# Attention into a two-layer feed-forward kernel: the first half step's product split into two stages, and the start-up issued in another order

## The chip, the cores and the metric

The kernel runs on one core of a Trainium2 chip. The metric is the device time of one execution in microseconds (us). TensorE is called PE, VectorE DVE, ScalarE ACT, GpSimd POOL, and SyncE, which issues the DMAs, SP. "SBUF" is the memory on the chip, "PSUM" the memory that PE writes.

## The reference, cut to what matters

```python
# q, k, v: (4, 8, 768, 64); mem_k, mem_v: (4, 8, 8, 64)
for c in range(24):                       # chunks of 32 tokens
    q_c = q[:, :, c_start:c_end]
    k_ctx = k[:, :, max(0, c_start - 16):min(S, c_end + 8)]
    k_full = concatenate([mem_k, k_ctx], axis=2)          # 64 keys
    scores = scale * q_c @ k_full.T
    a = exp(scores - max(scores)); a = a / (sum(a) + 1e-9)
    out[:, :, c_start:c_end] = a @ v_full
x = out.transpose(0, 2, 1, 3).reshape(3072, 512)
h = x @ w_in                              # 512 -> 2048
g = where(h >= 1, h, where(h <= -1, 0, (h + 1) ** 2 / 4))
return g @ w_out                          # 2048 -> 512
```

Everything is float32. The kernel gets that precision from PE by splitting x, g and the weights into a high and a low part (`hi`, rounded to a shorter format, and `lo`, the rest) and adding three products: high by high, high by low, low by high.

## The kernel before, in words

The 3072 tokens are six blocks of 512. For a block, attention makes x in SBUF as `xth` and `xtl` (high and low part, 512 features as four slices of 128 by 512 tokens). Then come 16 steps, one for each slice `fc` of 128 hidden columns: a *product* (`ps_h`, 12 matmuls: 8 that read `xth`, against the high and the low part of the weights, then 4 that read `xtl`), a *gate* (three ACT operations out of PSUM, a sum on DVE, a cast on ACT that gives the high part `gh`, a subtraction on DVE that gives the low part `gl`), and an *out* (`ps_o`, adding to the block's 512x512 result in four PSUM banks).

The first two blocks are issued by hand: `FIRST` (line 32) is a list of names, and for every name the loop at line 551 advances one generator by one stage, up to its next `yield`. Since every engine runs its instructions in the order of issue (`InOrder`, line 55), the list is the order on each engine; where a name stands matters only against other names with stages on the same engine. A wait on an engine therefore holds all that stands behind it there. The names are:

- `g0` to `g3` (`first_attention`, line 212): attention of block 0 in four groups, one for each half of the tokens (g0 and g1 the first half) and each half of the features (g0 and g2 the first two slices). The 13 stages: scores (PE, 64 matmuls), maximum, subtraction (DVE), exponential (ACT), row sum, +1e-9, reciprocal, multiplication (DVE), transposes (PE, 4), copy `pt` (ACT), values (PE, 64 matmuls), cast to `xth` (ACT), subtraction to `xtl` (DVE).
- `n0` to `n3` (`attention`, line 369): the same for the halves of blocks 1 and 2, all heads at once (128 matmuls each for scores and values); here the transposition is six DVE operations, and the scores and the values use one PSUM place, tag `s`, in turn. So n1's scores wait until n0's last subtraction to `xtl` has read it.
- `w0` to `w15` (`decode`, line 148): the weights come packed and are unpacked in place. Stages: scaling (ACT), shift, two merges (DVE), cast to the high part (ACT), subtraction to the low part (DVE). w0 holds the first two `fc` of w_in; w1 holds `fc` 2 of w_in and `fc` 0 of w_out, and so on.
- `A0` to `A3`, `B0` to `B3`: half steps of block 0, `fc` 0 to 3, for tokens 0 to 255 (A) and 256 to 511 (B); `J4` to `J15`: whole steps. C, D and E are the same for block 1. All are `early_step` (line 452), with the stages product, gate, sum, cast, subtraction, out (and stores after `fc` 15). A0 needs x of g0 and g1 only, B0 that of g2 and g3.
- `+`: the next load of the list `early` (line 530), on SP.

The products use a pool of two PSUM banks, `ps_h`, in the order of issue; g's transposes use it too. After `FIRST` a regular loop (line 573) runs blocks 2 to 5. What the change touches is `FIRST` and lines 464 and 465 in `early_step`.

Of the kernel before, what the change touches and what calls it, by code (L numbers as in the profile page):

```python
# [29 lines left out]


FIRST = """
    + + g0 g0 + g0 g1 g0 + g0 g1 g1 g0 g0 + g1 g0 w0 g1 g0 + g1 g1 g1 g0 w0 g1 + w0 g2 g1 w0 g1 g2 +
    w0 g2 w1 g0 w0 + g2 w1 g1 g2 + g0 g2 g2 g2 + g0 g2 w1 g3 g2 g1 w1 + A0 w2 g3 w1 g3 A1 w2 + g3 w1
    w3 g3 g2 A0 g3 g3 + A1 g3 A2 w2 g2 w4 g3 g2 A2 A0 w2 g3 A0 + g3 w3 w2 A0 w3 A0 g3 g3 + w2 B0 A1
    w3 A3 A1 B0 + A1 w3 B0 B1 w4 B0 w3 A3 A1 + B1 B0 w4 w5 B2 B1 w6 A2 w4 n0 + A2 B1 A2 w4 B1 A2 A3
    w5 A3 B2 + A3 w5 B3 w8 B2 w7 B0 w4 + B2 w5 B3 A3 w9 B2 B3 B1 w6 B3 + w5 w6 J4 w10 B3 w5 + w6 w11
    B2 w7 J4 w7 J5 + w6 w7 w12 w6 + w7 B3 J4 J5 w8 J6 w7 + J4 J5 w13 J4 w9 J5 J4 J6 w9 + J5 w15 J6
    w9 J7 J6 w14 J6 n0 w9 J5 J7 w9 w8 J7 J8 w8 J7 J7 w8 w11 J6 w8 J8 w11 J8 J9 w10 J8 w10 w11 J7 J9
    J8 w10 w11 J9 n0 w10 J10 J9 w10 n0 J9 w12 J8 J10 w12 w12 J11 J10 w12 w11 J10 J10 w13 J9 J11 w12  # L40
    w13 w14 J12 J11 n0 J11 n0 n0 J10 n0 J12 J11 n0 n0 J13 n0 n0 n0 n0 J11 w13 J13 J12 w13 J13 w14
    J12 n0 J13 w13 J12 J14 + n0 w14 n0 n0 w14 J12 w14 J14 J13 J14 w15 J14 n1 w15 w15 J15 + n1 w15
    w15 J13 J15 n1 J15 n1 J14 C0 J15 n1 J14 n1 n1 C0 n1 n1 J15 C1 n1 n1 J15 n1 C1 n1 n1 C1 C0 C1 C2
    J15 J15 C0 C1 n1 J15 J15 C0 C2 C2 C0 + n1 C2 n1 n1 C3 C2 C1 C3 C3 D0 C3 C3 C2 D0 D0 D1 D0 D0 n2
    D1 D1 D2 D1 + n2 C3 D1 D2 n2 D0 D2 n2 D2 D3 n2 D2 D1 n2 n2 D3 n2 E4 D3 n2 D3 n2 n2 n2 D2 E4 D3
    n2 E5 n2 E4 E4 E4 D3 E5 E6 E5 E5 E5 E4 E6 E6 E6 n2 E6 E7 + n2 n2 n2 n3 E7 E5 + n3 n3 E7 E8 n3 E7
    n3 n3 n3 E6 n3 E8 n3 n3 n3 E9 n3 n3 n3 E8 n3 E7 E8 E9 E8 E7 + n3 E9 E9 n3 n3 E9 E10 E8 E10 E10
    E10 E11 E10 E9 E11 E11 E11 E12 E11 E10 E12 E12 E12 E13 E12 E11 E13 E13 E13 E14 E13 E12 E14 E14
    E14 E15 E14 E13 E15 E15 E15 E15
"""  # L50

LAST = 2

# [15 lines left out]
def attn_ffn_kernel(ctx: ExitStack, tc: tile.TileContext, first_qk, first_v, qk, vw, w, out):  # L69
# [3 lines left out]
    NP = first_qk.shape[0]  # L73
# [9 lines left out]
    n2 = 2 * DM  # L83
# [10 lines left out]
    def two_banks(tag, name):  # L94
        return ps_2.tile([P, 2, 512], F32, name=name, tag=tag)
# [43 lines left out]
    def weights(which, fc, part):  # L139
        i, j = place[which, fc]  # L140
        c0 = part * n2 + j * DM
        return ws[i][:, c0 : c0 + DM]
# [250 lines left out]
    def hidden_terms(wh, wl, xh, xl):  # L393
        return [(m, x, cc) for m, x in ((wh, xh), (wl, xh), (wh, xl)) for cc in range(NP)]

    def pe_products(outs, gh, gl, wh, wl, fc):

        kinds = list(enumerate(((gh, wh), (gh, wl), (gl, wh))))
        todo = [(t, kind) for kind in kinds for t in range(len(outs))]
        if fc == NFC - 1:  # L400
            todo.sort(key=lambda x: x[0])
        for t, (i, (g, m)) in todo:
            ts = slice(t * P, (t + 1) * P)
            pe.matmul(outs[t], g[:, ts], m, start=fc == 0 and i == 0, stop=fc == NFC - 1 and i == 2)
# [47 lines left out]
    def early_step(name, blk, tokens, fc):  # L452

        items.append(name)
        size = len(tokens) * P
        xh, xl = (x[:, :, tokens[0] * P : tokens[0] * P + size] for x in xts[blk])
        n = 0
        if size < TB:
            n = len(halves) % 2
            halves.append(name)  # L460
        hp = ps_h.tile([P, 512], F32, name="ps_h")[:, 0:size]
        wh, wl = weights(0, fc, 0), weights(0, fc, 1)
        terms = hidden_terms(wh, wl, xh, xl)
        for i, (m, x, cc) in enumerate(terms):
            pe.matmul(hp, m[:, cc * P : (cc + 1) * P], x[:, cc], start=i == 0, stop=i == len(terms) - 1)
        yield
        if n == 0:
            tiles = (
                gpool.tile([P, TB], F32, name="gw", tag="gw"),
                gpool.tile([P, TB], F32, name="gt"),  # L470
                gpool.tile([P, TB], F32R, name="gh", bufs=3),
                gpool.tile([P, TB], F32R, name="gl", bufs=3),
            )
            if size < TB:
                both["g"] = tiles
        else:
            tiles = both["g"]
        g, t, gh, gl = (x[:, n * HT : n * HT + size] for x in tiles)
        act.activation(g, hp, AF.Relu, bias=0.5, scale=0.5)
        act.activation(t, hp, AF.Relu, bias=-1.0)  # L480
        act.activation(g, g, AF.Square)
        yield
        dve.scalar_tensor_tensor(g, g, 1.0, t, op0=ALU.min, op1=ALU.add)
        yield
        act.copy(gh, g)
        yield
        dve.tensor_tensor(gl, g, gh.bitcast(F32), op=ALU.subtract)
        yield
        if fc == 0:
            acc.setdefault(blk, [None] * NT)  # L490
            pair = two_banks(f"a{tokens[0] // 2}", "ps_o")
            for t in tokens:
                acc[blk][t] = pair[:, t % 2]
        wh, wl = weights(1, fc, 0), weights(1, fc, 1)
        pe_products([acc[blk][t] for t in tokens], gh, gl, wh, wl, fc)
        yield
        if fc < NFC - 1:
            return
        for t in tokens:
            if t % 2 == 0:  # L500
                ob = apool.tile([P, 2, DM], F32, name="ob", tag="f", bufs=2)
            (act.copy if t % 2 else dve.tensor_copy)(ob[:, t % 2], acc[blk][t])
            r0 = blk * TB + t * P
            sp.dma_start(out[r0 : r0 + P, :], ob[:, t % 2])
            yield
# [45 lines left out]
    for name in FIRST.split():  # L551
        if name == "+":
            load, *which = next(early)
            load(*which)
            continue
        if name not in chains:
            kind, i = name[0], int(name[1:])
            chains[name] = early_step(name, *parts[kind], i) if kind in parts else kinds[kind](i)
        next(chains[name])
# [13 lines left out]
    for s in range(first * NFC, steps):  # L573
# [30 lines left out]
        else:  # L604
            n, i = LAST // LAG, s - first * NFC
# [98 lines left out]
```

## Time and profile before

| | us |
|---|---|
| median of 3 runs | 608.17 (608.12 to 608.4) |
| the profiled execution | 608.17 |
| its span, first to last instruction | 606.4 |
| PE busy | 591.0 (97%) |
| DVE busy | 325.6 (54%) |
| ACT busy | 281.2 (46%) |

The shares are means over stages with different limits, so they don't say what bounds a stage; that is read from stretches and from waits. Nearly all instructions carry the line of the helper that records them, so they are told apart by what they write and read (`ps_x<-pt,v` are values) and by their place in time.

### The profile page before, as it was taken

How to read it: one execution, taken by the hardware profiler on the slowest of the kernel's cores; microseconds unless marked ns; L12 is line 12 of the kernel's file. 1: busy time of each engine (PE TensorE's matmuls, PEld its weight loads, DVE VectorE, ACT ScalarE, POOL GpSimd, SP SyncE). 2: the span in 40 equal slices, each digit the busy share in tenths (PEclk: the TensorE clock that was granted, in tenths of full speed). 3: DMA queues.
4: the chain of work that ended last, by engine and by line, in shares of the span. 5: the costliest groups of instructions: out<-in, count | busy, mean ns of one | idle time of the engine just before them, and what ended most of it. 6: DMA issues, size and time to landing. Idle time of an engine off the chain costs nothing.

```text
span 606.4 us, 12265 instructions
## 1 busy us (share of the span) xinstructions
PE 591.0 (97%) x5496; PEld 483.7 (80%) x5496; DVE 325.6 (54%) x466; ACT 281.2 (46%) x503; POOL 0.7 (0%) x6
## 2 busy tenths in 40 slices
PE   5889999999999999999999999999999999999996
PEld 2888888888888888888888888888888888888885
DVE  5999999987483224736424734623553632322222
ACT  2689764544444434344434434434433343533342
POOL 0000000000000000000000000000000000000000
PEclk8699999999999999999999999999999999999999
DMA  8999200433131004012201213101310000100001
GB/s 353 423 418 420 124 1 1 175 110 137 31 145 70 1 0 175 30 42 105 70 1 73 103 70 106 70 1 54 121 70 2 1 2 0 70 0 1 0 1 69
DMA packets 9845, 55.31 MB, mean 91 GB/s; under 512 B 1089, under 2 KB 1089, under 8 KB 5185
## 3 DMA queue, kind: packets, MB, share of 16 engines
q1 hardware_dynamic: 9792, 54.53, 23.2%
q8 instruction: 43, 0.70, 0.5%
q14 instruction: 10, 0.07, 0.0%
HBM read 48.23 MB, written 6.29 MB: 90 GB/s over the span
## 4 chain that ended last, share of the span: by engine, by line
PE 94%; DVE 3%; ACT 1%; DMA 1%; issue 0%; DVEq 0%; ACTq 0%
PE ps_o L63 44%; PE ps_h L63 44%; PE ps_x L63 3%; PE ps_s L63 3%; DVE f L63 1%; DMA qk<-in_first_qk_dram 1%; DVE pr L63 1%; DVE mx L63 0%; DVE den L63 0%; ACT w L63 0%; ACT gw L63 0%; DVE wr L63 0%; DVE xtl L63 0%; ACT pr L63 0%; ACT wr L63 0%
## 5 line engine op out<-in xcount | busy, mean ns | idle before, releaser
L63 PE MATMUL ps_o<-wr,gh 128*128 128x512 f32 x768 | 199.5, 396 | 0.0
L63 PE MATMUL ps_h<-xth,wr 128*128 128x512 f32 (+1 forms) x832 | 197.3, 379 | 0.0
L63 PEld LDWEIGHTS ps_h<-xth,wr 128*128 128x128 f32 x832 | 148.7, 189 | 31.9 <-DVE wr L63 0.5
L63 PEld LDWEIGHTS ps_o<-wr,gh 128*128 128x128 f32 x768 | 143.7, 188 | 32.5
L63 DVE SCALAR_TENSOR_TENSOR gw<-gw,gt 128x512 f32<-128x512 f32 (+1 forms) x104 | 67.2, 648 | 170.0 <-ACT gw L63 169.5
L63 ACT ACTIVATE gw<-ps_h 128x512 f32<-128x512 f32 (+1 forms) x104 | 58.7, 564 | 167.8 <-PE ps_h L63 167.7
L63 PE MATMUL ps_o<-wr,gl 128*128 128x512 f32 x384 | 109.0, 394 | 0.0
L63 PE MATMUL ps_h<-xtl,wr 128*128 128x512 f32 (+1 forms) x416 | 105.2, 375 | 0.0
L63 DVE TENSOR_TENSOR gl<-gw,gh 128x512 fp32r<-128x512 f32 (+1 forms) x104 | 67.4, 649 | 67.4 <-ACT gh L63 67.3
L63 ACT CAST gh<-gw 128x512 fp32r<-128x512 f32 (+1 forms) x104 | 61.1, 590 | 68.7 <-DVE gw L63 68.7
L63 PEld LDWEIGHTS ps_h<-xtl,wr 128*128 128x128 f32 x416 | 75.3, 190 | 14.1
L63 PEld LDWEIGHTS ps_o<-wr,gl 128*128 128x128 f32 x384 | 72.5, 189 | 17.2
L63 ACT ACTIVATE gw<-gw 128x512 f32<-128x512 f32 (+1 forms) x104 | 62.5, 601 | 0.0
L63 ACT ACTIVATE gt<-ps_h 128x512 f32<-128x512 f32 (+1 forms) x104 | 58.2, 559 | 0.0
L63 DVE STREAM_TRANSPOSE pt<-pr 32x512 f32<-32x512 f32 (+1 forms) x60 | 41.2, 698 | 1.3
L63 DVE SCALAR_TENSOR_TENSOR f<-w,f 128x1024 uint32<-128x1024 uint32 x32 | 38.9, 1220 | 0.4
L63 PEld LDWEIGHTS ps_x<-pt,v 64*64 64x64 f32 x1536 | 25.2, 142 | 5.5 <-issue 3.5
L63 ACT ACTIVATE pr<-pr 128x1024 f32<-128x1024 f32 (+1 forms) x14 | 13.1, 937 | 35.5 <-DVE pr L63 35.4
L63 PE MATMUL ps_x<-pt,v 64*64 64x32 f32 x1536 | 26.7, 226 | 1.6 <-ACT pt L63 1.6
L63 ACT CAST xth<-ps_x 128x512 fp32r<-128x512 f32 x24 | 13.1, 590 | 21.6 <-PE ps_x L63 21.5
L63 PEld LDWEIGHTS ps_s<-qk 64*32 64x32 f32 x1536 | 16.7, 110 | 6.4 <-issue 3.2
L63 ACT CAST wr<-f 128x1024 fp32r<-128x1024 f32 x16 | 16.8, 1050 | 9.3 <-DVE f L63 9.3
(27 smaller groups left out, 182.1 us busy)
## 6 DMA issues: line engine op xcount, KB each, us to landing
w<-in_w_dram SPq DMA_DIRECT2D x16, 1024.0 KB, 19.8
qk<-in_qk_dram SPq DMA_DIRECT2D x10, 1536.0 KB, 6.7
v<-in_vw_dram SPq DMA_DIRECT2D x10, 1024.0 KB, 5.1
out_dram<-ob SPq DMA_DIRECT2D x24, 256.0 KB, 2.0
qk<-in_first_qk_dram SPq DMA_DIRECT2D x4, 768.0 KB, 8.8
v<-in_first_v_dram SPq DMA_DIRECT2D x4, 512.0 KB, 12.8
```

Of the source, the lines that this page charges most:

```text
L63: return self.tc.keep_in_program_order(getattr(self.engine, name)(*args, **kwargs))
```

## The change

`early_step` gets one more `yield`, for the half step named A0 alone: its product is issued in two stages, the 8 matmuls that read the high part of x and the 4 that read the low part. `FIRST` is written anew, with 497 names for 496. The number and order of the loads on SP stay as they were. On PE the first steps come in this order:

| before | after |
|---|---|
| scores of g0, g1; transposes of g0, g1; scores of g2 | the same |
| values of g1, g0 | values of g0, g1 |
| transposes of g2 | A0 product, first 8 |
| scores of g3 | scores of g3 |
| A0 product (12) | A0 product, last 4 |
| A1 product | transposes of g2 |
| values of g2 | A1 product |
| A2 product | values of g2 |
| transposes of g3 | transposes of g3 |
| values of g3 | A2 product |
| A0 out | values of g3 |
| B0 product | A0 out, B0 product |
| A3, B1 products, A1 out, B2 product, scores of n0 | scores of n0, B1 product, A1 out, B2, A3 products |

On DVE the subtractions of g0 and g1 to `xtl` now stand ahead of g2's multiplication; g3's maximum and subtraction ahead of w1's second merge; and the rest up to n1 is interleaved anew. On ACT, A0's gate now stands ahead of g3's exponential and g2's copy `pt`. The values of n0 move behind J14's product, and n2's and n3's steps come later among those of E.

```diff
--- before.py
+++ after.py
@@ -30,24 +30,26 @@
 
 
 FIRST = """
-    + + g0 g0 + g0 g1 g0 + g0 g1 g1 g0 g0 + g1 g0 w0 g1 g0 + g1 g1 g1 g0 w0 g1 + w0 g2 g1 w0 g1 g2 +
-    w0 g2 w1 g0 w0 + g2 w1 g1 g2 + g0 g2 g2 g2 + g0 g2 w1 g3 g2 g1 w1 + A0 w2 g3 w1 g3 A1 w2 + g3 w1
-    w3 g3 g2 A0 g3 g3 + A1 g3 A2 w2 g2 w4 g3 g2 A2 A0 w2 g3 A0 + g3 w3 w2 A0 w3 A0 g3 g3 + w2 B0 A1
-    w3 A3 A1 B0 + A1 w3 B0 B1 w4 B0 w3 A3 A1 + B1 B0 w4 w5 B2 B1 w6 A2 w4 n0 + A2 B1 A2 w4 B1 A2 A3
-    w5 A3 B2 + A3 w5 B3 w8 B2 w7 B0 w4 + B2 w5 B3 A3 w9 B2 B3 B1 w6 B3 + w5 w6 J4 w10 B3 w5 + w6 w11
-    B2 w7 J4 w7 J5 + w6 w7 w12 w6 + w7 B3 J4 J5 w8 J6 w7 + J4 J5 w13 J4 w9 J5 J4 J6 w9 + J5 w15 J6
-    w9 J7 J6 w14 J6 n0 w9 J5 J7 w9 w8 J7 J8 w8 J7 J7 w8 w11 J6 w8 J8 w11 J8 J9 w10 J8 w10 w11 J7 J9
-    J8 w10 w11 J9 n0 w10 J10 J9 w10 n0 J9 w12 J8 J10 w12 w12 J11 J10 w12 w11 J10 J10 w13 J9 J11 w12
-    w13 w14 J12 J11 n0 J11 n0 n0 J10 n0 J12 J11 n0 n0 J13 n0 n0 n0 n0 J11 w13 J13 J12 w13 J13 w14
-    J12 n0 J13 w13 J12 J14 + n0 w14 n0 n0 w14 J12 w14 J14 J13 J14 w15 J14 n1 w15 w15 J15 + n1 w15
-    w15 J13 J15 n1 J15 n1 J14 C0 J15 n1 J14 n1 n1 C0 n1 n1 J15 C1 n1 n1 J15 n1 C1 n1 n1 C1 C0 C1 C2
-    J15 J15 C0 C1 n1 J15 J15 C0 C2 C2 C0 + n1 C2 n1 n1 C3 C2 C1 C3 C3 D0 C3 C3 C2 D0 D0 D1 D0 D0 n2
-    D1 D1 D2 D1 + n2 C3 D1 D2 n2 D0 D2 n2 D2 D3 n2 D2 D1 n2 n2 D3 n2 E4 D3 n2 D3 n2 n2 n2 D2 E4 D3
-    n2 E5 n2 E4 E4 E4 D3 E5 E6 E5 E5 E5 E4 E6 E6 E6 n2 E6 E7 + n2 n2 n2 n3 E7 E5 + n3 n3 E7 E8 n3 E7
-    n3 n3 n3 E6 n3 E8 n3 n3 n3 E9 n3 n3 n3 E8 n3 E7 E8 E9 E8 E7 + n3 E9 E9 n3 n3 E9 E10 E8 E10 E10
-    E10 E11 E10 E9 E11 E11 E11 E12 E11 E10 E12 E12 E12 E13 E12 E11 E13 E13 E13 E14 E13 E12 E14 E14
+    + + g0 g0 + g0 g1 g0 + g0 g1 g0 g0 g1 + g0 g1 w0 g1 g0 + g1 g1 g1 g0 w0 g1 + w0 g2 g1 w0 g0 g2 +
+    w0 g2 w1 g1 w0 + g2 w1 g0 g2 + g1 g0 A0 g2 g2 + g1 g2 g3 w1 A0 g3 + g2 g3 A0 w1 g3 A1 g2 g3 w1 +
+    g3 g3 g3 w2 g2 A0 w1 A1 g3 + g2 w2 A2 A0 g2 g3 A0 w4 w2 g3 A2 w2 A0 g3 + w3 g3 A2 B0 w2 A1 w3 A2
+    w3 A1 + n0 B0 w2 B1 B0 A1 + B0 w4 A1 w5 B0 w3 B1 B2 A2 + w3 w4 A3 B2 B1 w3 B1 w6 B3 + B2 B1 A3
+    w4 A2 B3 A3 w5 w4 + B0 w5 A3 B2 J4 w7 w4 w8 + B2 w6 w9 A3 B3 B1 w6 B3 J4 + w5 J5 w10 B3 J4 w5 w6
+    + B2 J4 w5 w11 A3 J4 J5 + w7 w7 B3 w12 w7 J6 w6 + J5 w13 w6 J5 n0 w7 + J4 w14 J5 w7 J6 + J7 w8
+    w15 J6 w8 J6 J6 J5 J7 w8 w9 w8 J7 w9 J8 J7 w9 w8 w9 J6 J8 J7 w10 w9 J9 w10 w11 w10 J7 J9 n0 J8
+    n0 J9 w11 J9 J10 J8 J9 w10 J8 n0 J8 J10 w10 n0 n0 w12 J10 J11 w11 J10 n0 w11 J10 J9 J11 w11 w12
+    J12 J11 w13 J11 w12 J11 w12 J10 w13 J12 w12 J12 J13 w13 J12 J12 w13 n0 n0 J11 J13 n0 w13 n0 J14
+    n0 n0 w15 J13 n0 w14 J13 w14 J14 J13 J12 + n0 w14 n0 n0 w14 w14 n1 J14 J15 w15 J14 + J14 w15 J13
+    n1 w15 J15 n1 w15 C0 n1 J15 J14 n1 C0 J15 C0 n1 n1 C0 J15 n1 C1 C0 n1 J15 C1 n1 n1 n1 n1 C2 n1
+    C1 n1 J15 J15 C1 C2 C1 J15 J15 C2 C3 + n1 C2 n1 n1 C0 C3 C2 D0 C3 C3 C3 C1 D0 D0 D1 D0 D0 C2 D1
+    D1 D2 D1 D1 C3 D2 D2 D3 D2 D2 D0 D3 D3 E4 D3 D3 D1 E4 E5 E4 E4 E4 D2 E5 E6 E5 E5 E5 D3 n2 E6 E4
+    E6 + n2 E6 E6 n2 E7 n2 n2 E5 E7 n2 n2 n2 E7 E8 n2 E7 n2 E7 n2 n2 E6 E8 n2 n2 E8 E8 n2 E8 E9 + n2
+    n2 n2 E7 E9 E9 E9 E10 E9 E8 E10 E10 E10 E11 E10 E9 E11 E11 E11 n3 E11 E10 + n3 n3 E12 n3 n3 n3
+    n3 E11 n3 E12 n3 n3 n3 E13 n3 n3 n3 E12 n3 E13 E12 E13 E14 + n3 E12 E13 n3 n3 E13 E12 E14 E14
     E14 E15 E14 E13 E15 E15 E15 E15
 """
+
+APART = "A0"
 
 LAST = 2
 
@@ -462,6 +464,8 @@
         wh, wl = weights(0, fc, 0), weights(0, fc, 1)
         terms = hidden_terms(wh, wl, xh, xl)
         for i, (m, x, cc) in enumerate(terms):
+            if name == APART and i == 2 * NP:
+                yield
             pe.matmul(hp, m[:, cc * P : (cc + 1) * P], x[:, cc], start=i == 0, stop=i == len(terms) - 1)
         yield
         if n == 0:
```

## Rows read from the trace of the kernel before

**Rows 1.** The page, part 1: busy time, share, instructions of an engine.

```profile
PE 591.0 (97%) x5496; PEld 483.7 (80%) x5496; DVE 325.6 (54%) x466; ACT 281.2 (46%) x503; POOL 0.7 (0%) x6
```

**Rows 2.** Waits of PE over the span: us in total, times, longest.

```profile
PE ps_h L63 <- DVE pr L63: 6.6, 3, 4.1
PE ps_x L63 <- ACT pt L63: 1.6, 1, 1.6
PE ps_s L63 <- DMA qk<-in_first_qk_dram: 1.4, 3, 0.8
```

**Rows 3.** Windows: stretch, its us, busy time by engine, granted clock, DMA share, GB/s.

```profile
15.00:20.00 5.00, 4.75 (x192) 4.45 (x192) 4.93 (x7) 3.54 (x6) 0.00 (x0) 0.50 1.02 421
...
26.00:26.50 0.50, 0.50 (x6) 0.50 (x5) 0.50 (x2) 0.50 (x2) 0.00 (x0) 0.77 1.20 475
...
8.45:128.16 119.71, 111.89 (x1247) 94.19 (x1248) 118.05 (x159) 78.81 (x133) 0.00 (x0) 0.93 0.54 221
...
128.90:601.00 472.10, 472.10 (x4107) 386.04 (x4107) 203.91 (x300) 199.26 (x366) 0.00 (x0) 1.00 0.15 53
```

**Rows 4.** Timeline of DVE: start us, us, operation, count.

```profile
20.76 0.69 DVE L63 TENSOR_TENSOR pr<-pr,rin 128x512 f32<-128x512 f32 x1
...
55.37 2.48 DVE L63 SCALAR_TENSOR_TENSOR f<-w,f 128x1024 uint32<-128x1024 uint32 x2
...
59.51 0.69 DVE L63 TENSOR_SCALAR f<-w 128x1024 uint32<-128x1024 uint32 x1
60.11 1.22 DVE L63 TENSOR_TENSOR wr<-f,wr 128x1024 fp32r<-128x1024 f32 x1
...
108.65 1.28 DVE L63 TENSOR_TENSOR xtl<-ps_x,xth 128x512 fp32r<-128x512 f32 x2
...
124.53 3.63 DVE L63 STREAM_TRANSPOSE pt<-pr 128x512 f32<-128x512 f32 x5
128.19 0.76 DVE L63 SCALAR_TENSOR_TENSOR gw<-gw,gt 128x256 f32<-128x256 f32 x2
...
175.26 4.24 DVE L63 STREAM_TRANSPOSE pt<-pr 128x512 f32<-128x512 f32 x6
```

**Rows 5.** Timeline of PE, from 108 us on.

```profile
111.90 1.48 PE L63 MATMUL ps_s<-qk 64*32 64x64 f32 x128
...
128.91 2.07 PE L63 MATMUL ps_x<-pt,v 64*64 64x32 f32 x128
...
179.59 2.07 PE L63 MATMUL ps_x<-pt,v 64*64 64x32 f32 x128
```

**Rows 6.** Timeline of PE, 16 to 36 us.

```profile
16.20 3.64 PE L63 MATMUL ps_x<-pt,v 64*64 64x32 f32 x128
21.59 1.08 PE L63 MATMUL ps_h<-ident,pr 128*128 128x128 f32 x4 [1.76 <-DVE pr L63]
22.61 1.19 PE L63 MATMUL ps_s<-qk 64*32 64x64 f32 x64
23.72 2.08 PE L63 MATMUL ps_h<-xth,wr 128*128 128x256 f32 x8
25.60 0.92 PE L63 MATMUL ps_h<-xtl,wr 128*128 128x256 f32 x4
26.36 1.11 PE L63 MATMUL ps_h<-xth,wr 128*128 128x256 f32 x8
...
29.05 1.22 PE L63 MATMUL ps_h<-xth,wr 128*128 128x256 f32 x8
...
35.34 1.11 PE L63 MATMUL ps_h<-xth,wr 128*128 128x256 f32 x8
```

**Rows 7.** Timeline of ACT, 19 to 29 us.

```profile
19.24 1.25 ACT L63 CAST xth<-ps_x 128x512 fp32r<-128x512 f32 x2
...
28.08 0.36 ACT L63 ACTIVATE gw<-ps_h 128x256 f32<-128x256 f32 x1
...
28.61 0.40 ACT L63 ACTIVATE gw<-gw 128x256 f32<-128x256 f32 x1
```

## The prediction

> **What bounds the kernel now.** The page comes first: TensorE (PE) is busy 591.0 of 606.4 us [rows 1], which leaves 15.4 us of idle time. The waits of PE say where: 6.6 + 1.6 + 1.4 = 9.6 us in three groups, for probabilities, for transposed probabilities and for the first loads [rows 2], all within the first 34 us; the rest is the first microsecond and the end of the program, where the last results are copied out. The stretches come next [rows 3]. From 128.90 to 601 PE is busy 472.10 of 472.10 us: nothing can be won there, except by reaching it sooner. But from 8.45 to 128.16 the vector engine (DVE) is full as well, 118.05 of 119.71 us, and what is missing is spacing between its operations, not waiting.
>
> So two engines are full at once, and the place where one holds the other is what counts. It is the values of n1. Their probabilities are transposed on DVE, the last five transpositions from 124.53 to 128.16 [rows 4]; PE starts n1's values at 128.91 [rows 5], 0.75 us after. Everything that stands ahead on DVE has to be done by then, in either order. A PE that is several us early at 36 us gives all of it back at n1's values unless DVE ends sooner too. The prediction is therefore a sum on DVE, with a check that nothing new makes DVE wait.
>
> **The change, part by part.** No instruction is added or removed: A0's twelve matmuls become eight (those that read the high part of x) and four, with g3's scores between. Four parts.
>
> *The front on PE.* Now A0's product starts at 23.72, behind g2's transposes (21.59) and g3's scores (22.61), and PE is idle for 1.76 us ahead of them [rows 6]. In the new order its first eight follow g0's and g1's values, which end at 19.84 (16.20 + 3.64). The second cast of x's high part ends at 19.24 + 1.25 = 20.49 [rows 7]; two matmuls need only the first cast. At 1.2 GHz one takes (25.60 - 23.72) / 8 = 0.235 us. So: two from 19.9, six from 20.6, done at 22.0; g3's scores (1.19) to 23.2; the last four to 24.0; g2's transposes (1.08) to 25.1; A1 from 25.0. Putting the full clock at 26.2, as now (the stretch 26.00 to 26.50 has 0.77, that is a rise near 26.2 [rows 3]), A1's product, of which eight matmuls take 1.11 at 2.4 GHz [rows 6], ends near 27.2, g2's values near 28.3, and B0's product starts near 33.0 against 35.34 with the same work behind it: PE is 2.3 us ahead. Two more changes between small and full tiles on PE cost between 0 and 0.1 us each: eight matmuls behind g2's values take 1.22 (at 29.05), behind others 1.11 [rows 6]. I take 0, since 2.3 us of lead cover either end.
>
> *The front on DVE.* The subtractions of g0 and g1 now stand ahead of g2's multiplication, and w1's merges and subtraction come later. What could now make DVE wait are three hand-overs. g3's maximum: DVE comes free for it at 23.42 (the multiplication at 20.76 [rows 4] moves to 21.67 behind two subtractions, then 0.69 and one merge of 1.22, each overlapping its neighbour by 0.08); g3's scores end at 23.2, and 0.12 us later DVE could start: slack 0.1. g3's row sum: ScalarE (ACT) first does A0's three gate operations, 0.93 us from 28.08 to 28.61 + 0.40 in the trace [rows 7], here from 24.1, then g3's exponential to 25.6; DVE is busy until 25.9: slack 0.3. g2's low part: the cast of its values on ACT is done near 29.5, DVE is free at 29.7: slack 0.2. All three are met, none by much. What is queued behind on ACT (g2's copy, w1's cast, w2's scaling, then A1's gate) slips only if A0's last four matmuls do.
>
> *The whole way to n1's values on DVE.* Before, 146 operations lie between w0's shift and n1's last transposition. 35 of the pairs of neighbours are spaced by +0.03 us (the second needs the first's result, or one is a late transposition, as in the pair that takes 2.48 for two of 1.22 to 1.23), and 110 overlap by 0.08 (59.51 + 0.69 = 60.20, next start 60.11) [rows 4]. After, there are 148: C0's sum and C0's subtraction now stand ahead of the last transposition, 0.42 us each (a pair of this size takes 0.76 with its overlap [rows 4]); and the new order interleaves more, 28 pairs of the first kind and 119 of the second. The difference: 0.84 - 7 x 0.034 - 9 x 0.078 = -0.10 us, and 0.05 more from the same effect ahead of w0's shift. The last transposition ends at 128.16 - 0.15 = 128.0, and PE starts 0.14 us behind it (as at 21.59 after 20.76 + 0.69 = 21.45 [rows 4, 6]): 128.15 instead of 128.91, a gain of 0.76 us. A second route gives no later time: n1's scores need n0's low part, whose end moves from 109.93 (108.65 + 1.28) to 110.8 by the same count (net 1.38 more of durations, 0.49 less of spacing, and the 0.05), so they start at 110.9 instead of 111.90 and n1's values, 17.01 us behind on PE, could start at 127.9 [rows 4, 5].
>
> The size of the spacing is the one place here where a rule speaks against the change. The trace shows 0.03 and -0.08 [rows 4]. The Trainium skill, page "VectorE: DVE Perf Modes", section "The DRAIN you can't avoid", says that the next operation cannot start until the pipe is empty and that a semaphore between two operations costs nothing extra; by that, interleaving saves nothing, only the two added operations would be left, and the time would be that of rival 2. The trace differs from it, by 0.11 us per pair, and I go by the trace.
>
> *The later part.* From n1's values to 217 us only the order of n2's and n3's steps against E's changes. PE is full there, and DVE is busy 203.91 of 472.10 us [rows 3]. n3 is the tight one: its last six transpositions end at 175.26 + 4.24 = 179.50 and PE starts its values at 179.59 [rows 4, 5]; after the change the same four E steps cover the same chain, so between 0 and 0.1 us, taken as 0. The loads that wait for n3's scores and values go out some 25 us later by the order of the steps; more than ten steps of PE work, each longer than the 1.11 of those eight matmuls, lie between them and their first use, so they cost nothing; without that cover it would be a landing each. The order of issue on SP itself is unchanged, and so are POOL's few instructions.
>
> **The sum.** The profiled execution took 608.17 us, the median of the runs, of which 606.4 are its span. 608.17 - 0.76 = **607.4 us**. A measurement of this kernel can tell about 0.2% (1.2 us) from no change; this gain is under that.
>
> **Rivals.**
> 1. *The clock comes late* (slower). Between 15 and 20 us PE is busy 4.75 of 5.00 us, with g2's scores and the values of g0 and g1, and the granted clock is 0.50 all the while, 1.2 GHz [rows 3]. The rise to 2.4 GHz near 26.2 follows A0's twelve matmuls and A1's first ones with nothing between; after the change eight, g3's scores, four, g2's transposes and then A1. If the clock stays at 1.2 GHz until about 29.5, A1's product takes 12 x 0.235 = 2.8, g2's values 1.8 (half of 3.64), and g2's cast ends near 30.3: DVE waits 0.7 for g2's low part, and 608.1 is left. From there on each further us lands on DVE; if it stays until 33, A2's product and g3's values are slow too, DVE waits 2.9 in all: **610.3**. For it: what PE does ahead of 26.2 is cut into more pieces than before. Against it: from 20.6 on PE has hardly a gap, a microsecond sooner than now (21.59 [rows 6]). Chance 0.14 for 608.1, 0.06 for 610.3.
> 2. *Interleaving saves nothing on DVE.* Then the two operations cost 2 x (0.42 - 0.05) = 0.7 net and n1's values start at 129.0: **608.3**. Against it: the two kinds of neighbours in the rows above. Chance 0.11.
> 3. *DVE is not the bound.* If the 0.75 us at n1's values were chance and DVE could give way, PE's whole lead of 2.3 would last: **605.9**. Against it: DVE's 118.05 of 119.71. Chance 0.07.
> 4. *The change does not do what it says*: A0's first stage starts only when both casts are done and further waits cost it half a us, ending at 22.5. g3's scores end at 23.7 and DVE waits 0.4 for its maximum: **607.8**. Chance 0.12.
>
> **How the numbers follow.** The forecast, 607.2 to 607.7 in its own range (the run-to-run spread of 0.3 and the small hand-overs), has 0.48; 0.02 is left for slower cases that I have not named. The range 606.9 to 608.7 holds the forecast, rivals 2 and 4 and the first price of rival 1, 0.85 together, and leaves out rival 3 and the late end of rival 1. Faster by over 0.2% (under 606.95): rival 3 and the lower edge of the forecast, 0.09. Slower by over 0.2% (over 609.4): 0.08. Within: 0.83.
>
> **What the profile will show.** Right: A0's eight matmuls on PE near 20 us, before g3's scores; DVE still without a wait over 0.2 us from 8.45 on; PE short waits (a few tenths) somewhere between 95 and 128 us, where there were none, because its lead runs into DVE; n1's values starting at 128.1 to 128.3; PE full from there. Wrong: n1's values before 127.5 (DVE is not what I took it for), a wait of DVE for ACT or PE between 23 and 35 us (rivals 1 and 4), a granted clock of 0.50 beyond 27 us (rival 1), or any PE gap after 130 us (the later part).

## The result and the profile after

The changed kernel takes **610.94 us**, the median of 5 runs (609.97 to 611.43), against 608.12 (607.97 to 608.4) before: the ratio is 1.0044, 95% interval 1.0031 to 1.0057. It is slower, and beyond the forecast's range. The profiled execution took 609.97 us, the fastest of the five: 1.80 us over the profiled 608.17 of before. The account below is for these 1.80 us; what the other four lost beyond that has no profile.

The page, parts 1 and 3 of the changed kernel (engines; queue: packets, MB, share):

```profile
PE 591.2 (97%) x5496; PEld 483.3 (79%) x5496; DVE 324.9 (53%) x466; ACT 280.9 (46%) x503; POOL 0.7 (0%) x6
...
q8 instruction: 43, 0.70, 0.5%
```

PE's work is what it was [rows 1]. The second line is one that I had not read. By its size queue 8 carries PE's own program: 0.70 MB for 5496 matmuls and 5496 weight loads is 64 bytes each; in 43 packets that is 16 KB, or 256 instructions, per packet.

The waits of PE, and those of DVE from 8.45 us to n1's last transposition, changed kernel:

```profile
PE ps_h L65 <- DVE pr L65: 4.6, 2, 3.8
PE ps_o L65 <- issue: 3.0, 1, 3.0
...
PE ps_x L65 <- issue: 1.2, 1, 1.2
```

```profile
DVE gw L65 <- ACT gw L65: 2.7, 2, 2.4
```

The waits for probabilities are down from 6.6 to 4.6 us and the one for transposed probabilities (1.6) is gone [rows 2]. New are 3.0 and 1.2 us for "issue", which means that PE waited for nothing that the profile shows, and 2.7 us (2.37 and 0.31) in which DVE waits for a gate: before, DVE had no wait of that kind ahead of 128 us.

The timeline of PE, changed kernel, 19 to 43 us and around n1:

```profile
19.70 2.41 PE L65 MATMUL ps_h<-xth,wr 128*128 128x256 f32 x8
22.05 1.06 PE L65 MATMUL ps_s<-qk 64*32 64x64 f32 x64
23.04 0.74 PE L65 MATMUL ps_h<-xtl,wr 128*128 128x256 f32 x4
...
28.29 0.43 PE L65 MATMUL ps_x<-pt,v 64*64 64x32 f32 x16 [1.24 <-issue]
...
33.23 1.12 PE L65 MATMUL ps_h<-xth,wr 128*128 128x256 f32 x8
34.18 0.64 PE L65 MATMUL ps_h<-xtl,wr 128*128 128x256 f32 x4
34.75 1.82 PE L65 MATMUL ps_s<-qk 64*32 64x64 f32 x128
...
38.03 0.40 PE L65 MATMUL ps_o<-wr,gh 128*128 128x512 f32 x1
41.39 0.97 PE L65 MATMUL ps_o<-wr,gh 128*128 128x512 f32 x3 [2.96 <-issue]
...
113.45 1.47 PE L65 MATMUL ps_s<-qk 64*32 64x64 f32 x128 [0.38 <-issue]
...
130.47 2.07 PE L65 MATMUL ps_x<-pt,v 64*64 64x32 f32 x128
...
135.39 1.11 PE L65 MATMUL ps_h<-xth,wr 128*128 128x256 f32 x8
136.48 0.74 PE L65 MATMUL ps_h<-xtl,wr 128*128 128x256 f32 x4
```

Down to 33.23 this is nearly the order and the times of the forecast. Then n0's scores (34.75) take the place that B1's product had, and within A1's output product, between its first matmul and its second, stand 2.96 us of idle time. Windows of the changed kernel, and of the one before for the same stretch:

```profile
22.00:23.00 1.00, 1.00 (x65) 0.90 (x64) 1.00 (x2) 0.00 (x0) 0.00 (x0) 0.59 1.02 426
23.00:24.00 1.00, 1.00 (x21) 0.93 (x8) 0.96 (x3) 0.19 (x1) 0.00 (x0) 1.00 1.00 418
36.00:50.00 14.00, 11.04 (x123) 9.85 (x111) 11.29 (x18) 9.14 (x21) 0.00 (x0) 1.00 1.01 418
```

```profile
36.00:50.00 14.00, 14.00 (x210) 12.67 (x210) 14.00 (x23) 12.88 (x28) 0.00 (x0) 1.00 1.01 418
```

From 36 to 50 us both engines were full before; now both miss 2.7 to 3 us. DVE stands still because B2's gate comes late, and that because B2's product is queued on PE behind the idle time. From there on DVE carries the delay to n1, as these lines of its timeline show (n0's low part, n1's six transpositions):

```profile
112.07 1.28 DVE L65 TENSOR_TENSOR xtl<-ps_x,xth 128x512 fp32r<-128x512 f32 x2
...
126.23 4.24 DVE L65 STREAM_TRANSPOSE pt<-pr 128x512 f32<-128x512 f32 x6
```

n0's low part ends at 113.35 (109.93 before [rows 4]), n1's scores start at 113.45 (111.90 [rows 5]), n1's values at 130.47 (128.91): **1.56 us**. Between those scores and those values PE has no gap in either kernel, 17.0 us in both. (The "issue" ahead of n1's scores is this wait for n0's low part, 0.10 us behind its end; the word alone is no proof of a missing instruction.) The other 0.24 come right after: D0's product lasts from 135.39 to 137.22, 1.83 us, where B0's same twelve matmuls take 1.59 (33.23 to 34.82); its last four, at 136.48, read n1's low part, which ends on DVE at 136.43. 1.56 + 0.24 = 1.80.

### The profile page after: what moved, and what is told of

The parts are those of the page before. It is cut to its first block, busy times and chain, and to the rows that moved or that the text cites. A ratio compares the mean times of both kernels' runs of the same rounds, so it can differ in the third digit from the quotient of the medians.

```text
span 608.2 us, 12262 instructions
## 1 busy us (share of the span) xinstructions
PE 591.2 (97%) x5496; PEld 483.3 (79%) x5496; DVE 324.9 (53%) x466; ACT 280.9 (46%) x503; POOL 0.7 (0%) x6
## 3 DMA queue, kind: packets, MB, share of 16 engines
q1 hardware_dynamic: 9792, 54.53, 23.2%
## 4 chain that ended last, share of the span: by engine, by line
PE 96%; DMA 2%; issue 1%; SPq 0%; ACT 0%; DVE 0%; DVEq 0%; ACTq 0%
PE ps_h L65 45%; PE ps_o L65 44%; PE ps_x L65 4%; PE ps_s L65 3%; DMA qk<-in_first_qk_dram 2%; SPq L65 0%; DVE ob L65 0%; ACT gw L65 0%; ACT ob L65 0%; DVEq L704 0%; ACT gt L65 0%; ACTq L65 0%
## 5 line engine op out<-in xcount | busy, mean ns | idle before, releaser
L65 PE MATMUL ps_s<-qk 64*32 64x64 f32 x1536 | 19.2, 235 | 2.0 <-DMA qk<-in_first_qk_dram 1.5
```

The lines of the kernel that those rows point to most:

```text
L65: return self.tc.keep_in_program_order(getattr(self.engine, name)(*args, **kwargs))
```

## The experiments

**What stops PE in A1's output product.** Its operands were there: the last two, w2's and A1's low parts, ended on DVE at 37.23 and 37.90, before the product began:

```profile
36.01 1.22 DVE L65 TENSOR_TENSOR wr<-f,wr 128x1024 fp32r<-128x1024 f32 x1
...
37.48 0.42 DVE L65 TENSOR_TENSOR gl<-gw,gh 128x256 fp32r<-128x256 f32 x1
```

My theory is the supply of instructions. n0's scores are 128 matmuls with 128 weight loads, a whole packet of program in 1.5 us. From the stop at 28.29 to the stop at 41.39 PE runs 16 matmuls of g2's values, 4 transposes, 12 (A2), 64 (g3's values), 6 (A0's output), 12 (B0), 128 (n0), 12 (B1) and 1: 255, with their loads 510 instructions, which is two packets. The rival is that the place of n0's scores, or something that they wait for, costs. The traffic of the changed kernel around the gap (DMA view; the first line is the stretch of 34 to 38.8 us, the others that of 38.8 to 40; queue, packets, MB, share):

```profile
q1 hardware_dynamic: 280, 2.03, 100.9%
...
q1 hardware_dynamic: 62, 0.48, 98.2%
q8 instruction: 1, 0.02, 5.7%
```

One packet of program comes at 38.85 to 39.94, none in the 4.8 us before, while the loads of weights keep the transfer engines at 98 to 101%. PE goes on at 41.39, 1.45 us after it has landed.

*Undo the place alone* (n0_late): n0's scores go behind B3's product.

```diff
-    w3 A1 + n0 B0 w2 B1 B0 A1 + B0 w4 A1 w5 B0 w3 B1 B2 A2 + w3 w4 A3 B2 B1 w3 B1 w6 B3 + B2 B1 A3
+    w3 A1 + B0 w2 B1 B0 A1 + B0 w4 A1 w5 B0 w3 B1 B2 A2 + w3 w4 A3 B2 B1 w3 B1 w6 B3 n0 + B2 B1 A3
```

> The changed kernel with one name of the list moved: n0's scores (256 PE instructions, 1.5 us) go behind B3's product instead of behind B0's. Theory 1, the instruction supply: PE's program comes by DMA in packets of 16 KB; the profile counts 43 of them (0.70 MB) for some 11,000 PE instructions, so one holds 256. In the changed kernel PE resumes behind each of two gaps (1.24 us at 28.29, 2.96 us at 41.39) about 1.4 us after such a packet has landed, and n0's scores alone use up a packet. By this theory the 2.96 us gap goes, DVE has no wait over 0.3 us between 9 and 125 us, n1's values start at 128.1 to 128.4, and the time is 607.3 to 607.9. Theory 2, a wait for data in A1's out that the profile does not name (w2's low part, A1's low part, a PSUM bank): the gap stays with A1's out, near 3 us, and the time is 610 to 611.5.

608.06 us (607.75 to 608.6), ratio to the kernel before 1.0001 (0.9992 to 1.001). The 2.96 us gap is gone, and with it all of the loss; but the kernel is level with the one before, not under it. Theory 1 was right about the gap and too low in the time (607.3 to 607.9): n1's values start at 128.73, not at 128.1 to 128.4.

*That place alone, in the kernel before* (before_n0_early):

```diff
-... g3 g3 + w2 B0 A1 w3 A3 ... w6 A2 w4 n0 + A2
+... g3 g3 + w2 B0 n0 A1 w3 A3 ... w6 A2 w4 + A2
```

> The kernel before with one name moved: n0's scores go right behind B0's product, as the changed kernel has them. Theory 1 (instruction supply): the packet for the instructions behind n0's scores lands near 41 to 43 us as before, so PE stands still for 3 to 5 us from about 38.5 on; PE had no idle time from 34 us on, so nearly all of it shows: 610.5 to 613 us. Theory 2 (a data wait in the new order around A1's out): nothing happens, 607.9 to 608.5.

611.64 us (611.42 to 611.93), ratio 1.0058 (1.0044 to 1.0072). The timeline of PE in this kernel has the same gap in another product, between the first and the second of twelve matmuls:

```profile
39.79 0.28 PE L63 MATMUL ps_h<-xth,wr 128*128 128x256 f32 x1
42.33 1.10 PE L63 MATMUL ps_h<-xth,wr 128*128 128x256 f32 x7 [2.26 <-issue]
```

The gap is shorter than the 3 to 5 us expected; behind it PE waits 0.62 and 0.18 us more, for a gate and for a weight, and 3.5 us are lost in all. So the loss goes with n0's scores, without any other part of the change, and it falls on whatever product the count of instructions reaches: counted by their starts, the same 1462 matmuls and weight loads lie ahead of the gap here as in the changed kernel, though in another order. The changed kernel's first stop lies behind 953 of them, 509 fewer (one of the 510 loads and matmuls counted above had begun ahead of that stop).

*Keep the order, empty the queues* (loads_held): from w6 on the weights' loads wait until A1's low part is done, by a write to w6's buffer.

```diff
-    ... B0 w2 B1 B0 A1 + B0 w4 A1 ...
+    ... B0 w2 B1 B0 A1 hold + B0 w4 A1 ...
...
+    held = const.tile([P, 1], F32, name="held", tag="w_6")
     for name in FIRST.split():
+        if name == "hold":
+            dve.memset(held, 0.0)
+            continue
```

> The changed kernel, n0's scores where the change put them, but the load of w6 and all loads behind it on SP wait until A1's low part is done on DVE (37.9 us), by a one-column tile that shares w6's place. The loads before it are through by about 35 us, so the DMA engines are nearly idle from 35 to 38 us. Theory 1 (instruction supply): the packet asked for near 35.2 us no longer queues behind data for 3.6 us, starts within about 1 us, and the 2.96 us gap shrinks to under 0.6 us; weights still come in time (w6 is scaled at 45 us); 607.3 to 608.3. Theory 2 (data wait on PE): the gap stays, and later weights can only cost: 610 to 612.

DMA view, 36 to 37.4 us, and PE's timeline:

```profile
q1 hardware_dynamic: 20, 0.13, 22.2%
q8 instruction: 1, 0.02, 4.3%
```

```profile
37.75 0.40 PE L65 MATMUL ps_o<-wr,gh 128*128 128x512 f32 x1
38.69 0.50 PE L65 MATMUL ps_o<-wr,gh 128*128 128x512 f32 x1 [0.55 <-issue]
```

With the loads down to 22% of the engines the same packet comes at 36.34, 2.5 us sooner, and the gap in the same product is 0.55 instead of 2.96 us. The gap is as expected (under 0.6); the time, 609.86 us (ratio 1.003, 1.0018 to 1.0041), is not (607.3 to 608.3), and is no answer to the question: the held weights arrive late (ACT waits 1.02 and 1.33 us for them) and make PE and DVE wait elsewhere.

*Keep the place, halve the instructions* (half_scores): the changed kernel, but 64 of n0's 128 products stay there and 64 go behind B3's product (the function that issues them takes the half to issue).

```diff
-    ... B1 w3 B1 w6 B3 + B2 B1 A3
+    ... B1 w3 B1 w6 B3 n0 + B2 B1 A3
...
-        pe_scores(key)
+        if key == (1, 0):
+            pe_scores(key, range(2))
+            yield
+            pe_scores(key, range(2, NP))
+        else:
+            pe_scores(key)
```

> The changed kernel, with the moved scores of the first quarter n0 in two halves: 64 of the 128 products stay behind B0's product, 64 go behind B3's. Same work in all. Theory (PE runs out of instructions, which come 256 at a time): the instruction at which the 2.96 us gap stands is reached 128 instructions later in PE's program, and the products that follow use only 24 instructions in 1.4 us, so the next packet is there long before: no gap over 0.3 us in A1's output product, 607.5 to 608.3. Rival (what costs is that the scores, or their wait, stand at this place at all): half of the gap or more stays, 609.3 or more.

607.76 us (607.31 to 608.12), ratio 0.9993 (0.9984 to 1.0002): 3.2 us under the changed kernel, not clear of the one before. A1's output product runs through:

```profile
34.73 0.86 PE L65 MATMUL ps_s<-qk 64*32 64x64 f32 x64
...
37.05 1.27 PE L65 MATMUL ps_o<-wr,gh 128*128 128x512 f32 x4
38.26 0.74 PE L65 MATMUL ps_o<-wr,gl 128*128 128x512 f32 x2
...
110.91 1.47 PE L65 MATMUL ps_s<-qk 64*32 64x64 f32 x128 [0.31 <-issue]
...
127.90 2.07 PE L65 MATMUL ps_x<-pt,v 64*64 64x32 f32 x128
```

```profile
109.53 1.28 DVE L65 TENSOR_TENSOR xtl<-ps_x,xth 128x512 fp32r<-128x512 f32 x2
...
123.69 4.23 DVE L65 STREAM_TRANSPOSE pt<-pr 128x512 f32<-128x512 f32 x6
```

Same place, same work, half the instructions at once: no gap. Place and operands are ruled out; the count decides. This kernel is also the nearest to the change as I had forecast it: n0's low part ends at 110.81, n1's scores start at 110.91, the last transposition ends at 127.92.

**What the split is worth.** *A0's product in one piece*, behind g3's scores, else as n0_late (no_split):

```diff
-APART = "A0"
+APART = ""
```

(with the first of the two A0 taken out of the order that issues them).

> The kernel of e1_n0_late without the split: A0's twelve matmuls together, behind g3's scores. My account of the front says that the first eight filled PE time in which g3's scores could have run, and that A0's last matmul ends near 23.8 either way: the time is that of e1_n0_late within 0.4 us. If the split itself is what carries the front (an earlier full clock, an earlier gate), this is slower than e1_n0_late by more than 1 us.

609.26 us (609.07 to 610.3), ratio 1.0022 (1.0013 to 1.0031): 1.2 us more than with the split, and my account was wrong again for the same reason. PE's timeline:

```profile
19.73 0.45 PE L65 MATMUL ps_s<-qk 64*32 64x64 f32 x13
21.88 1.06 PE L65 MATMUL ps_s<-qk 64*32 64x64 f32 x51 [1.70 <-issue]
```

g3's scores stop after 13 of 64. In the changed kernel the eight matmuls of the first stage, 16 instructions in 2.4 us, lie in just this time. A packet landed at 20.57, 1.31 us before they go on, and 698 instructions lie ahead of the stop, 255 fewer than ahead of the changed kernel's first. The split pays, but as a filler that needs few instructions. An earlier full clock, the expectation's other reason, does not account for it: the granted clock rose earlier with the split (within 24 to 25 us in n0_late, 25 to 26 here), but A0's product was nearly over by then in both (24.52 and 25.70), and the 1.70 us stop is more than the 1.18 between these ends.

**Why n0_late is not faster.** Its front is 0.84 us later than that of half_scores by B0's product (34.05 against 33.21), where the two programs are the same. PE stops in g2's values, for 1.32 us; in half_scores it stops there for 0.33 (until 28.05). The packet for these instructions began at 26.66 in one execution and at 25.62 in the other; why, stays open. And where n0's scores filled PE's time in the changed kernel, it now waits for DVE, for w2's low part. Its timeline of PE:

```profile
29.11 0.43 PE L65 MATMUL ps_x<-pt,v 64*64 64x32 f32 x16 [1.32 <-issue]
...
36.92 0.63 PE L65 MATMUL ps_o<-wr,gh 128*128 128x512 f32 x2
37.98 0.73 PE L65 MATMUL ps_o<-wr,gh 128*128 128x512 f32 x2 [0.43 <-DVE wr L65]
```

The next four kernels go from here. *DVE brings w2's low part earlier* (decode_after_hand_over): one step of w3's decoding goes behind A1's low part.

```diff
-    A2 w3 A1 + B0 w2 B1 B0 A1 +
+    A2 A1 + B0 w2 B1 B0 A1 w3 +
```

> The run with n0's scores behind B3's product (608.06, no gap left), with one DVE step of w3's decoding (its second, 1.22 us) moved behind A1's low part, so that w2's low part and the sums of B0 and A1 come 1.2 us earlier. Theory (PE lost its lead of 1.3 us between 36 and 58 us to DVE's hand-overs, w2's low part first; from 58 us it has no gap in either kernel): the 0.43 us wait for w2's low part goes, PE is 0.5 to 1.2 us earlier at B3's product, but n1's scores stay at 111.6, because n0's low part is then last; 607.8 to 608.1. Rival (PE alone bounds it, the whole lead reaches the end): 606.9 to 607.4.

608.17 us, ratio 1.0 (0.9991 to 1.0009). The wait for w2's low part is gone, and PE waits in A3's and B3's products instead, for ACT to have read the accumulator that they take:

```profile
39.89 1.22 PE L65 MATMUL ps_h<-xth,wr 128*128 128x256 f32 x8 [0.52 <-ACT gt L65]
...
42.06 1.21 PE L65 MATMUL ps_h<-xth,wr 128*128 128x256 f32 x8 [0.46 <-ACT gt L65]
```

*C0's hand-over back behind n1's transpositions* (c0_behind_transposes), as in the kernel before:

```diff
-    J15 C0 n1 n1 C0 J15 n1 C1 C0 n1 J15 C1 n1 n1 n1 n1 C2 n1 C1
+    J15 n1 n1 J15 n1 C1 n1 J15 C1 n1 n1 n1 n1 C2 n1 C0 C0 C1 C0
```

> The run with n0's scores behind B3's product, with the sum and the low part of C0 on DVE behind n1's transpositions, where the kernel before has them, so that n1's transpositions end about 0.69 us earlier. If DVE alone sets n1's values (as the prediction had it): 607.3 to 607.5, n1's values at 128.1. If PE is full from 58 us on and DVE only keeps pace with it: n1's values stay within 0.15 of 128.73 and the time is 607.9 to 608.2.

608.54 us, ratio 1.0009 (1.0 to 1.0018): neither theory's time. n1's values start 0.68 us earlier in its trace (128.05), but n1's scores are as much earlier (111.05 for 111.72), and B0's product before them (32.80 for 34.05, at the same instructions), so the edit itself moved nothing there. *Both, and w15's first decoding step behind n0's low parts* (both), that is the two diffs above and

```diff
-    n0 w15 J13 n0 w14 J13 w14 J14 J13 J12 + n0 w14 n0 n0 w14 w14 n1
+    n0 J13 n0 w14 J13 w14 J14 J13 J12 + n0 w14 n0 n0 w15 w14 w14 n1
```

> Both of the last two edits, and w15's first decoding step (0.69 us) behind n0's low parts. Theory (from 36 to 128 us both engines are full, so a gain needs room on both): n0's low part at about 111.0, n1's scores at 111.1, n1's values at 128.1 to 128.3, 607.3 to 607.6, under both of its parts and under the kernel before. If the time is within 0.2 of 608.06, something else holds n1's values or D0's product.

608.86 us, ratio 1.0014 (1.0005 to 1.0023): worse, so something behind n1's values takes more than the edits give. Timelines of PE and ACT in c0_behind_transposes:

```profile
128.05 2.07 PE L65 MATMUL ps_x<-pt,v 64*64 64x32 f32 x128
...
133.24 1.22 PE L65 MATMUL ps_h<-xth,wr 128*128 128x256 f32 x8
134.56 0.74 PE L65 MATMUL ps_h<-xtl,wr 128*128 128x256 f32 x4
```

```profile
132.10 1.08 ACT L65 CAST xth<-ps_x 128x512 fp32r<-128x512 f32 x2
```

n1's values end at 130.12, and ACT copies them only at 132.10: ahead of the copies stand C2's gating and a copy of block 0's output, which itself waits for DVE. D0's product reads these copies and the low parts behind them. It starts late and lasts 2.06 us instead of 1.60.

*The copies and low parts of n1 first* (n1_low_first), else as c0_behind_transposes:

```diff
-    C0 n1 J15 J15 C1 C2 C1 J15 J15 C2 C3 + n1 C2 n1 n1 C0 C3 C2 D0
+    C0 n1 J15 J15 C1 n1 C2 C1 J15 n1 n1 J15 C2 C3 + C2 C0 C3 C2 D0
```

> The run with C0 behind n1's transpositions, with n1's two copies on ACT ahead of C2's gating and of the last copy of block 0's output (they now stand behind both), and n1's low parts on DVE ahead of C2's sum. In that run n1's values began at 128.05, 0.68 earlier than without C0's move, but the copies only at 132.10, 2.0 us after the values had ended, D0's product waited inside for the low parts (2.06 us for 1.60) and 0.5 of the 0.68 was gone. Theory (this hand-over is where a lead at n1's values is lost): copies at 130.4 to 130.6, D0's product in 1.6 to 1.65 us without a wait, 0.5 to 0.9 us less than that run's 608.54: 607.5 to 608.0. If it isn't: 608.3 to 608.7.

608.14 us, ratio 0.9998 (0.9989 to 1.0007). PE's timeline:

```profile
128.85 2.07 PE L65 MATMUL ps_x<-pt,v 64*64 64x32 f32 x128
...
133.78 1.11 PE L65 MATMUL ps_h<-xth,wr 128*128 128x256 f32 x8
134.73 0.64 PE L65 MATMUL ps_h<-xtl,wr 128*128 128x256 f32 x4
```

D0's product takes 1.59 us: its wait, the 0.24 us of the changed kernel, is gone. From n1's values to the end this trace loses 0.12 us against the kernel before, c0_behind_transposes 0.86. The time fell by 0.4 us, less than the 0.5 expected, and the two intervals overlap; in this execution all is 0.8 us later than in the other as far as n1's values.

*Together, but without w3's step* (halves_and_n1_low_first): the changed kernel with n0's scores in two halves, C0's hand-over, w15's step and n1's copies moved, by the diffs above.

> All that the runs so far found, in one kernel: the changed kernel with n0's scores in two halves (607.76), C0's sum and low part behind n1's transpositions, w15's first decoding step behind n0's low parts, and n1's copies and low parts as in the run beside this one. Theory (three limits in a row: PE's instructions, then n0's low part and n1's transpositions on DVE, then n1's low parts on ACT and DVE ahead of D0's product): n1's scores at 110.4 to 110.8, n1's values at 127.3 to 127.7, no wait in D0's product, 606.9 to 607.5. If D0's product does not limit, no better than 607.76.

**607.31 us** (606.67 to 607.74), ratio to the kernel before 0.9985 (0.9976 to 0.9994): under both kernels.

```profile
110.60 1.48 PE L65 MATMUL ps_s<-qk 64*32 64x64 f32 x128
...
127.61 2.07 PE L65 MATMUL ps_x<-pt,v 64*64 64x32 f32 x128
...
132.53 1.12 PE L65 MATMUL ps_h<-xth,wr 128*128 128x256 f32 x8
```

n1's scores, n1's values and D0's product (132.53, without a wait) are each where the expectation had them. How much of the 0.87 us each edit brings was not taken apart.

## Why the prediction was wrong

**What failed** is the step "the check that nothing new makes DVE wait". I held every moved step against what it reads and against the engine that runs it. The move of n0's scores from 42.60 to 34.75 stands in the table of the change but in none of the prediction's four parts: to me it was 1.48 us of PE work in another place, covered by "2.3 us of lead". It is also 256 instructions. The missing term is PE's supply of program: 2.96 us of idle PE, of which DVE lost 2.37 + 0.31 waiting for gates. n1's values lost 1.56 of it; the rest is what the new order gains there (1.01 in half_scores, 127.90 for 128.91), to about 0.1. In the kernel before PE meets the same scores at 42.60 without a wait. The sign that could have been read is a line of the page, queue 8, and that its packets come 6.3 to 7.3 us apart while the loads run (from 19.93 to 47.24 us in the kernel before).

**The front on PE** was right in order and nearly in time: eight matmuls at 19.70 to 22.11 (19.9 to 22.0), g3's scores to 23.11 (23.2), the last four to 23.78 (24.0), B0's product at 33.23 (33.0). Two errors in it cancel: the clock, which I left at 26.2, rose to 2.4 GHz within 22 to 23 us (0.59, then 1.00), with PE at work without a gap from 15.0 on, and g2's values stopped for 1.24 us at 27.05, the same lack of instructions. That the clock rose so early is luck: with the same order up to there, also without a gap from 15.2 on, it rose within 24 to 25 us in n0_late (0.84) and half_scores (0.66), and after 26 in n1_low_first (0.50 from 25 to 26). What sets the moment stays open. **Rival 1** (a clock later than 26.2) did not occur in the changed kernel.

**The front on DVE**: the three hand-overs were met; DVE's first new wait is at 42.9 us.

**The sum on DVE** was right in its times, and half_scores shows them, where no long gap disturbs: last transposition 127.92 (forecast 128.0), n0's low part 110.81 (110.8), n1's scores 110.91 (110.9). But the link on which the 0.76 us rest, that n1's values wait for the last transposition, is not there. No trace shows PE waiting at n1's values: they start 17.0 us behind n1's scores in every kernel (128.91 behind 111.90 before, 127.90 behind 110.91 in half_scores, there 0.02 us ahead of the transposition's end), and before the change PE had no wait at all from 34 us on. The 0.75 us between them was slack. What DVE holds is n1's scores, which wait for n0's low part (0.38 us in the changed kernel, 0.31 in half_scores): the second route, whose 127.9 was met. That half_scores' 607.76 us is near the forecast's 607.4 is in part luck: in its trace n1's values gain 1.01 us instead of 0.76, and 0.37 are lost behind them, where the forecast has nothing.

**Rival 2** asked for n1's values at 129.0 and fell: the two added operations did not push the last transposition past 127.92 in half_scores. The Trainium skill's rule beside it ("VectorE: DVE Perf Modes", "The DRAIN you can't avoid") is half of what that section says: it goes on that an operation which is not held starts earlier, and the prediction left that out. No run here tests which operations are held.

**The later part** was mis-sized: "between 0 and 0.1 us" measured 0.24. I had looked at the loads and at n3 there, not at who reads n1's low parts first: one output product fewer now lies between n1's values and D0's product, and ACT's order has the copies behind other work.

**Rival 3** (DVE is not the bound) was right that the 0.75 us at n1's values were no bound: in c0_behind_transposes DVE was 0.4 us early there (last transposition 127.65) and nothing came of it. It was wrong that PE's whole lead would last: without the long gap 607.76 was left, not 605.9. From 36 to 128 us both engines are nearly full, and a gain needs room on both and in the hand-over behind them. **Rival 4** did not occur: A0's first stage started at 19.70.

**Open**: why the median of the changed kernel lies 0.97 us over its profiled execution, and what makes the same packet of program and the rise of the clock come a microsecond or more earlier or later from one execution to the next.

## What to carry to other kernels

When a step moves, count its instructions as well as its time: short matmuls with a weight load each use up program far faster than long ones (here 256 instructions in 1.5 us against 24 in 1.5). While loads kept the transfer engines full, PE got a packet of 256 only every 6 to 7 us (starts at 19.38, 25.85, 32.83, 38.85 and 45.05 us in the changed kernel), so leave that much long work between two such bursts, or split the burst. And a wait for "issue" in the middle of one product, whose neighbours run on the same operands, is the mark of it.

## What was not expected of the hardware

PE's program arrives by the same transfer engines as the data. With these at 98 to 101% a packet took 1.0 to 1.1 us and began 2.2 to 4.9 us after PE had entered the last one it had (starts of packets between 19 and 48 us against the count of instructions; the kernel before, the changed kernel and half_scores); at 22% it was 1.4 us. Where PE had stopped, it went on 1.3 to 1.5 us after the landing. The Trainium skill, page "Runtime: NRT & Kernel Launch", section "Instruction fetch mechanics", has the blocks of 16 KiB, or 256 instructions, each fetched while the one before it runs, and calls the cost of crossing into the next "mostly hidden". The traces agree with the size (stops behind 698, 953 and 1462 instructions, in whichever kernel) and with the fetch one block ahead. Most crossings cost nothing here too, but not all: 1.24 and 2.96 us in the changed kernel, 2.26 in before_n0_early, 1.70 in no_split.
